# Attention feeding a SiLU feed-forward layer: the keys loaded a second time as plain rows, their root moved into exp's scale, the queries' root and row scaling moved from VectorE to GpSimd

## The chip, the cores and the metric

The kernel runs on one core of a Trainium2 chip. A core has a matrix engine (TensorE, PE in the profile, with its weight loads as PEld), three engines for elementwise work (VectorE = DVE, ScalarE = ACT, GpSimd = POOL) and queues that start DMA transfers (SyncE = SP issues nearly all of them here). Each engine works through its own instruction list strictly in order; engines wait for each other through semaphores. The metric is the device time of one execution in microseconds (us). Three runs of the kernel before gave 1366.65 to 1367.55 us, with a median of 1367.14 us.

## The reference

Inputs are `q`, `k`, `v` of 8 batches x 12 heads x 448 positions x 64, two gain vectors of 64, and two weight matrices of 768 x 2048 and 2048 x 768, all float32.

```
q_n = q / sqrt(mean(q*q, -1) + 1e-6) * g_q        # likewise k_n with g_k
scores = q_n @ k_n.T / sqrt(64)                   # per batch and head
attn = softmax(scores)                            # over the keys
x = (attn @ v), heads side by side                # 3584 x 768
h = x @ w_in ;  g = h * sigmoid(h) ;  out = g @ w_out
```

A query row's root is a factor common to a row of the scores; a key row's root is a factor common to a column. With the keys of one block lying on the 128 partitions, as the scores are computed here (transposed, keys on partitions, queries along the free dimension), the root of a key is one number per partition.

## The kernel before, in words

**Groups.** Four heads (two pairs) of one batch make a group `c`; there are 24 (`NC`), and six of them (`GROUP = 6`) cover two batches. The main loop in `bounded` alternates `visit(c)`, the attention matmuls of a group, and `between(c)`, the preparation of the next group together with two "fills". A fill (`fill`, line 1302) issues matmuls of the first feed-forward product for two batches already finished, done as seven products instead of eight (`Seven`, lines 856 to 893: sums of the inputs, sums of the results), and deals other work (`others`, `prompt`) out between these matmuls at even distances. After the last group a long tail does the rest of the feed-forward products; attention and fills take the first 770 us or so.

**Order.** Everything is under a manual schedule: the instruction order on each engine is the order of the Python calls. PSUM tiles of `scores` and of `scale` come from one pool `sc` with two buffers, each used by the next that asks; those of the products from a pool `mm` with two.

**Early groups (c < 6).** Keys are loaded as plain rows (`load_k`). `normalise` squares them on ACT, sums on DVE (`Norm.squares`, lines 449 and 450), and `Norm.root` makes `1/sqrt` with one DVE instruction (line 474) and a power by POOL (line 478, exponent -0.5). The keys' root is not multiplied into the rows: line 712 gives it to ACT's exp as its scale, one number per partition. The transposes run on PE.

**Late groups (c >= 6), on which the change bears.** q and k are loaded as 32-wide "quarters" (`load_quarters`, line 245, eight DMAs each), so that DVE can transpose them by 32 x 32 blocks (`flip`, lines 636 and 639). For a group c+1 this happens before:

- `sum_squares` (lines 654, 655): ACT squares 128 x 896, DVE sums 28 columns, once for q, once for k; the sums hold half a head each.
- `scale(c + 1)` (lines 660 to 686), called in the middle of `visit(c)`: a small PE matmul adds the two halves (line 664; `ident` was altered by `pair_up` for that), DVE adds epsilon (line 665), then a Newton iteration for the reciprocal root on DVE, ten instructions on 128 x 56 (lines 669 to 678), then two DVE multiplications of 128 x 896 (line 686), which scale the rows of q and of k in place.
- in `between(c)`: `flip(c + 1, "q")` first, then during the second fill `flip(c + 1, "k")` and `gain`, which multiplies by the gains on ACT (line 645).

Exp's scale is then the constant 1.0. Per late group DVE also adds the weights of the softmax (`add`, line 758), inverts the sums (line 787) and combines products (line 828); during groups 5 to 10 it converts and sums pieces of `w_in` too (lines 124 to 131 and 825/828), with POOL's addition on line 135.

The line that the change alters in the exp, and the place where `scale` stood:

```
scale=norm.column(c, i, h, j) if c < GROUP else 1.0,     # line 714, in scores
if GROUP - 1 <= c < NC - 1 and c != GROUP:               # line 1404, in visit
    scale(c + 1)
```

Of the kernel before, what the change touches and what calls it, by code (L numbers as in the profile page):

```python
# [23 lines left out]


SCORE_MAX = 60.0

RSQRT_START = float(0x5F375A86)

BANK = 512  # L30

# [160 lines left out]
def kernel(  # L192
# [60 lines left out]
    def load_q(c, t, steps=1):  # L253
# [7 lines left out]
        for i in range(steps):  # L261
            n = 4 // steps
            dst = t[0:R, ts(i, nq // steps)].rearrange("p (n j d) -> p n (j d)", n=n, j=J)
            nc.sync.dma_start(dst, rows[ts(i, n)].rearrange("n (p j) d -> p n (j d)", j=J))

    def load_k(c):
        t = place[f"k{c % 2}"]
        if c >= z.NPAIR:
            b, cp = divmod(c, z.NPAIR // 2)
            load_quarters(k[b, ts(cp, 4)], t)  # L270
            return
        main, left = keys_of(k, c)
        for i, start in enumerate((z.KA, z.KB)):
            dst = t[:, ds(start, z.KL)].rearrange("p (j h d) -> p j h d", j=z.KEYS, h=2)
            nc.sync.dma_start(dst, main[:, ts(i, 2)].rearrange("p h j d -> p j h d"))
            if i == 0:
                for m in range(2):
                    dst = t[ds(m * z.LEFT, z.LEFT), ds(z.KL, 2 * D)]
                    nc.sync.dma_start(dst.rearrange("p (h d) -> p h d", h=2), left[m])

    def plain_v(c, i):

        b, cp = divmod(c, z.NPAIR // 2)
        rows = v[b, ds(4 * cp + 2 * i, 2)]
        start = i * z.LEFT
        main = rows[:, ds(start, z.KEYS * P)].rearrange("h (j p) d -> p h j d", p=P)
        return main, rows[:, ds((1 - i) * z.KEYS * P, z.LEFT)].rearrange("h p d -> p h d")

    def load_v(c):
        if c >= z.NPAIR:  # L290
            dst = place["v"].rearrange("p (i h j d) -> p i h j d", i=2, h=2, d=D)
            for i in range(2):
                for h in range(2):
                    source = plain_v(c, i)[0][:, h, 0 : z.KEYS - 1]
                    nc.sync.dma_start(dst[:, i, h], source)
            return
        main, _ = keys_of(v, c)
        dst = place["v"].rearrange("p (n j d) -> p n j d", n=4, j=z.KEYS - 1)
        nc.sync.dma_start(dst, main[:, :, 0 : z.KEYS - 1])

    def load_v_rest(c):
        if c >= z.NPAIR:
            for i in range(2):
                main, left = plain_v(c, i)
# [12 lines left out]
    loads = {"q": load_q, "k": load_k, "v": load_v, "vrest": load_v_rest}  # L317

    pairs = [(b, hp) for b in range(z.B) for hp in range(z.NPAIR)]

# [9 lines left out]


    room = Room(nc, const, w_in, z)
    rms = [const.tile([P, 56], F32, name=f"rms{i}") for i in range(2)]
# [97 lines left out]
class Norm:  # L431
# [3 lines left out]
    def __init__(self, nc, z, rms, minus_half):  # L435
        self.nc, self.z, self.rms, self.minus_half = nc, z, rms, minus_half
        self.nq = 2 * z.J

        self.at = [(2 * self.nq, 2 * z.KEYS + 2), (2 * self.nq + 2 * z.KEYS + 2, 2 * z.KEYS)]

    def column(self, c, i, h, j):

# [75 lines left out]
def bounded(  # L518
# [100 lines left out]
    def transpose_k(c):  # L619


        assert z.KB == BANK
        t = ps.tile([P, 2, BANK], F32, name="sc", bufs=2)
        rows = place[f"k{c % 2}"]
        for i in range(2):
            for j in range(z.KEYS + 1 - i):
                nc.tensor.transpose(t[:, i, ts(j, P)], rows[:, ds((z.KA, z.KB)[i] + j * P, P)], ident)
        columns = t.rearrange("p i s -> p (i s)")[:, 0 : z.NK]
        nc.scalar.activation(kT, columns, AF.Copy, scale=gains)
        if c + 2 < NC:  # L630
            loads["k"](c + 2)

    def flip(c, name):

        if name == "q":
            nc.vector.transpose(qT.rearrange("p i s -> p (i s)"), q_of(c)[:, 0 : z.NK])
            load_q(c + 1)
            return
        nc.vector.transpose(kT, place[f"k{c % 2}"])
        if c + 2 < NC:  # L640
            loads["k"](c + 2)

    def gain():

# [1 line left out]

    n = z.NK // z.Q

    def sum_squares(c, name):

        if c >= NC:
            return
        rows = q_of(c)[:, 0 : z.NK] if name == "q" else place[f"k{c % 2}"]
        nc.scalar.activation(squares, rows, AF.Square)  # L654
        nc.vector.tensor_reduce(  # L655
            out=norm.rms[c % 2][:, ts("qk".index(name), n)],
            in_=squares.rearrange("p (n e) -> p n e", e=z.Q), axis=AX.X, op=ALU.add,
        )

    def scale(c):  # L660

        f = norm.rms[c % 2][:, 0 : 2 * n]
        t = ps.tile([P, 2, BANK], F32, name="sc", bufs=2)[:, 0, 0 : 2 * n]
        nc.tensor.matmul(t, ident, f, start=True, stop=True)
        nc.vector.tensor_scalar(
            out=f, in0=t, scalar1=1.0 / D, scalar2=1e-6, op0=ALU.mult, op1=ALU.add
        )
        y, a = (squares[:, ts(i, 2 * n)] for i in range(2))
        nc.vector.tensor_scalar(
            out=y.bitcast(I32), in0=f.bitcast(I32), scalar1=-0.5, scalar2=RSQRT_START,  # L670
            op0=ALU.mult, op1=ALU.add,
        )
        for i in range(3):
            nc.vector.tensor_tensor(out=a, in0=f, in1=y, op=ALU.mult)
            nc.vector.scalar_tensor_tensor(
                out=a, in0=a, scalar=-0.5, in1=y, op0=ALU.mult, op1=ALU.mult
            )
            nc.vector.scalar_tensor_tensor(
                out=f if i == 2 else y, in0=a, scalar=1.5, in1=y, op0=ALU.add, op1=ALU.mult
            )  # L680
        for i, name in enumerate("qk"):
            rows = q_of(c)[:, 0 : z.NK] if name == "q" else place[f"k{c % 2}"]
            rows = rows.rearrange("p (n e) -> p n e", e=z.Q)
            factor = f[:, ts(i, n)]
            factor = factor.rearrange("p (n one) -> p n one", one=1).to_broadcast([P, n, z.Q])
            nc.vector.tensor_tensor(out=rows, in0=rows, in1=factor, op=ALU.mult)

    def pair_up():

# [8 lines left out]
    def scores(c, j, i=None):  # L698
# [12 lines left out]
        for h in range(2):  # L711
            nc.scalar.activation(  # L712
                eleft[:, h] if j == LEFT else weights(c, j)[:, i, h], two[:, h, 0:S], AF.Exp,
                scale=norm.column(c, i, h, j) if c < GROUP else 1.0,
            )

    def turn(step, copy):
# [88 lines left out]
    def normalise(c):  # L806


        def piece(name, i):
            if name == "q":  # L810
                norm.squares_q(c, raw_of(c), scratch[i], i)
                norm.root(c, name, i)
                norm.scale(c, raw_of(c), q_of(c), i, nc.gpsimd)
                if i == 1 and c + 2 < GROUP:
                    load_q(c + 2)
            else:
                norm.squares_k(c, place[f"k{c % 2}"], scratch[i], i)
                if i == 1:
                    norm.root(c, name)

        return [lambda a=a: piece(*a) for a in (("q", 0), ("q", 1), ("k", 0), ("k", 1))]


# [539 lines left out]
    def visit(c):  # L1363

        if c < GROUP - 1:
            beside = normalise(c + 1)
        elif c <= GROUP:
            beside = [lambda: sum_squares(c + 1, "q")]
        else:
            beside = []  # L1370
        if c < NC:
# [29 lines left out]
                loads["vrest"](c + 1)  # L1401
        if c == NC:
            return
        if GROUP - 1 <= c < NC - 1 and c != GROUP:
            scale(c + 1)
        scores(c, 1, 0)
        scores(c, 1, 1)
        if c < GROUP:
# [2 lines left out]
        scores(c, 2, 0)  # L1411
        weigh(c, 1, 1)
        turn(0, nc.scalar.copy)
        if c == GROUP:
            scale(c + 1)
        if c < GROUP:
            run_all(beside[3:4])
        scores(c, 2, 1)
# [11 lines left out]
    def between(c):  # L1430
# [38 lines left out]
        if c % GROUP == GROUP - 1:  # L1469
# [247 lines left out]
```

## Time and profile before

| what | value |
|---|---|
| median of three runs | 1367.14 us |
| the profiled execution's own time | 1367.57 us |
| its span, first to last instruction | 1365.7 us |
| mean granted TensorE clock | 0.991 of full speed |
| PE busy | 1308.2 us, 96% |
| DVE busy | 1017.1 us, 74% |
| ACT busy | 476.5 us, 35% |
| POOL busy | 202.3 us, 15% |
| bytes moved by DMA | 139.42 MB |

"Busy" is the union of an engine's instructions. A group of instructions is given by line, engine and operation, with the tile written, the tiles read, their shapes, the count, then the busy time and the mean duration; after a second bar stands the idle time of the engine just before these instructions, and what ended it. The matrix engine's matmuls are pipelined and overlap in the records, so four matmuls of 64 x 64 on different parts of the array count once; an idle PE is a real loss, while a busy one isn't a proof of full speed.

### The profile page before, as it was taken

How to read it: one execution, taken by the hardware profiler on the slowest of the kernel's cores; microseconds unless marked ns; L12 is line 12 of the kernel's file. 1: busy time of each engine (PE TensorE's matmuls, PEld its weight loads, DVE VectorE, ACT ScalarE, POOL GpSimd, SP SyncE). 2: the span in 40 equal slices, each digit the busy share in tenths (PEclk: the TensorE clock that was granted, in tenths of full speed). 3: DMA queues.
4: the chain of work that ended last, by engine and by line, in shares of the span. 5: the costliest groups of instructions: out<-in, count | busy, mean ns of one | idle time of the engine just before them, and what ended most of it. 6: DMA issues, size and time to landing. Idle time of an engine off the chain costs nothing.

```text
span 1365.7 us, 19617 instructions
## 1 busy us (share of the span) xinstructions
PE 1308.2 (96%) x7111; PEld 811.8 (59%) x7111; DVE 1017.1 (74%) x1810; ACT 476.5 (35%) x859; POOL 202.3 (15%) x169
## 2 busy tenths in 40 slices
PE   8988898899999999999999999999999999999998
PEld 4333333334344444344444455556999999999998
DVE  5787987787766666776665667679887787878785
ACT  7864445454444444444444234420000000000000
POOL 6751111121001000100100134430000000000000
PEclk9998999999999999999999999999999999999999
DMA  9564355433333333333331247531413232323311
GB/s 243 146 149 111 75 134 141 100 77 79 97 85 76 78 100 77 97 78 79 78 91 46 99 130 236 185 123 43 128 45 126 73 97 74 102 76 101 112 59 38
DMA packets 252558, 139.42 MB, mean 102 GB/s; under 512 B 190436, under 2 KB 236388, under 8 KB 252452
## 3 DMA queue, kind: packets, MB, share of 16 engines
q1 hardware_dynamic: 251888, 137.09, 36.0%
q8 instruction: 58, 0.95, 0.3%
q0 software_dynamic: 256, 0.79, 0.2%
q14 instruction: 48, 0.39, 0.1%
q10 hardware_dynamic: 308, 0.20, 0.1%
HBM read 88.47 MB, written 41.29 MB: 95 GB/s over the span
## 4 chain that ended last, share of the span: by engine, by line
PE 50%; DVE 1%; issue 0%; ACT 0%; ACTq 0%; DVEq 0%
PE alone L1177 22%; PE mm L870 8%; PE mm L1177 7%; PE alone L870 7%; PE alone L1214 2%; PE av L744 1%; PE sc L707 1%; PE mm L1214 1%; DVE work L828 0%; PE sc L778 0%; DVE x L828 0%; DVE x L802 0%; DVE rows L825 0%; DVE sums_x L825 0%; DVE work L787 0%
## 5 line engine op out<-in xcount | busy, mean ns | idle before, releaser
L870 PE MATMUL mm<-x,W 128*128 128x448 f32 x636 | 260.9, 552 | 17.3 <-DVE parts L828 8.1
L870 PEld LDWEIGHTS mm<-x,W 128*128 128x128 f32 x636 | 118.1, 192 | 152.2 <-issue 116.7
L870 PE MATMUL mm<-sums_x,W 128*128 128x448 f32 x456 | 185.9, 547 | 5.1 <-DVE stage L828 3.8
L707 PE MATMUL sc<-work 64*64 64x448 f32 x1344 | 163.6, 555 | 14.4 <-ACT work L712 10.1
L712 ACT ACTIVATE work<-sc 128x448 f32<-128x448 f32 x252 | 122.4, 540 | 113.5 <-PE sc L707 90.2
L744 PE MATMUL av<-work,rows 64*64 64x448 f32 x1296 | 147.1, 543 | 7.3 <-DVE av L720 4.3
L870 PEld LDWEIGHTS mm<-sums_x,W 128*128 128x128 f32 x456 | 85.6, 191 | 97.6 <-issue 84.7
L758 DVE TENSOR_TENSOR work<-work 128x896 f32<-128x896 f32 (+1 forms) x114 | 124.0, 1111 | 8.3 <-PE av L744 7.7
L890 POOL TENSOR_TENSOR parts<-parts,stage 128x448 f32<-128x448 f32 x31 | 41.5, 1340 | 489.6 <-DVE parts L828 489.6
L1177 PE MATMUL alone<-W,rows 128*128 128x192 f32 x608 | 113.0, 326 | 0.0
L707 PEld LDWEIGHTS sc<-work 64*64 64x64 f32 x1344 | 46.8, 134 | 97.5 <-issue 31.4
L1177 PEld LDWEIGHTS alone<-W,rows 128*128 128x128 f32 x608 | 101.2, 190 | 0.0
L744 PEld LDWEIGHTS av<-work,rows 64*64 64x64 f32 x1296 | 51.5, 134 | 83.5 <-issue 45.1
L1177 PE MATMUL alone<-W,work 128*128 128x192 f32 x382 | 72.2, 326 | 0.0
L787 DVE RECIPROCAL work<-sc 128x224 f32<-128x224 f32 x36 | 55.7, 1549 | 18.9 <-PE sc L778 18.9
L1008 ACT ACTIVATE stage<-stage 128x896 f32<-128x896 f32 x63 | 57.3, 945 | 34.3 <-DVE stage L828 33.6
L505 POOL DMA_DIRECT2D out_dram<-x x2 | 1.3, 652 | 443.2 <-DVE x L828 443.2
L1177 PEld LDWEIGHTS alone<-W,work 128*128 128x128 f32 x382 | 63.8, 190 | 0.0
L655 DVE TENSOR_REDUCE rms<-rows 128x28 f32<-128x896 f32 x36 | 39.0, 1082 | 31.7 <-ACT rows L654 31.7
L1187 ACT COPY rows<-alone 128x192 f32<-128x192 f32 x34 | 10.8, 318 | 137.5 <-PE alone L1177 79.0
L870 PE MATMUL alone<-x,W 128*128 128x448 f32 x132 | 53.7, 551 | 1.4 <-DVE x L802 1.4
L1191 ACT COPY rows<-alone 128x192 f32<-128x192 f32 x34 | 10.8, 319 | 123.1 <-PE alone L1177 119.6
(248 smaller groups left out, 2144.1 us busy)
## 6 DMA issues: line engine op xcount, KB each, us to landing
hidden<-stage SPq DMA_DIRECT2D x63, 448.0 KB, 2.8
work<-hidden SPq DMA_DIRECT2D x21, 1024.0 KB, 5.1
rows<-in_moe_w_out_dram SPq DMA_DIRECT2D x32, 384.0 KB, 3.4
W<-in_moe_w_in_dram SPq DMA_DIRECT2D x22, 512.0 KB, 4.6
work<-work SPq DMA_DIRECT2D x144, 56.0 KB, 1.9
rows<-in_q_dram SPq DMA_DIRECT2D x144, 56.0 KB, 2.2
rows<-in_k_dram SPq DMA_DIRECT2D x144, 56.0 KB, 2.3
x<-hidden SPq DMA_DIRECT2D x7, 1024.0 KB, 5.5
```

The costliest lines, as they stand in the source:

```text
L655: nc.vector.tensor_reduce(out=norm.rms[c % 2][:, ts("qk".index(name), n)], in_=squares.rearrange("p (n e) -> p n e", e=z.Q), axis=AX.X, op ...
L707: nc.tensor.matmul(two[ds(half * D, D), h, 0:S], keys[rows, ts(half, D)], qT[rows, pair, :], start=True, stop=True,)
L712: nc.scalar.activation(eleft[:, h] if j == LEFT else weights(c, j)[:, i, h], two[:, h, 0:S], AF.Exp, scale=norm.column(c, i, h, j) if c < ...
L744: nc.tensor.matmul(sums[i][ds(h * D, D), :], v, w, start=(j == 0 and step == 1), stop=(j == LEFT - 1 and step == 1),)
L758: nc.vector.tensor_tensor(out=total, in0=total, in1=more, op=ALU.add)
L787: nc.vector.reciprocal(out=r[0][:, rows], in_=t[:, rows])
L870: nc.tensor.matmul(t, self.left(name, s), self.right(name, s), start=s == ends[0], stop=s == ends[1])
L890: nc.gpsimd.tensor_tensor(out=u2, in0=u2, in1=p5, op=ALU.add)
L1008: nc.scalar.activation(t, t, AF.Silu)
L1177: nc.tensor.matmul(t, x[:, i], y, start=i == ORDER[0], stop=i == ORDER[-1])
L1187: nc.scalar.copy(p1, product(1))
L1214: nc.tensor.matmul(o, a[:, 2 * i + m, t], right_one(name, i)[:, m], start=n == 0, stop=n == len(steps) - 1,)
```

## The change

For late groups the keys are now kept twice. The raw quarters go to the buffer `k1` (`load_k_quarters`) and are transposed unscaled; the plain rows go to `k0` (`load_k`, new branch), where only their squares are taken, with the early groups' functions, and their root becomes exp's scale. `scale` now does q alone: matmul and epsilon as before, then POOL's power and POOL's multiplication of the rows; the Newton chain is gone. `scale(c + 2)` is called at the end of `between(c)` instead of `scale(c + 1)` within `visit(c)`. The key's squares for c + 2 stand last in the first fill, behind all softmax additions, where the sum of the k quarters stood between them before.

```
-            load_quarters(k[b, ts(cp, 4)], t)
+            t = place["k0"]
+            for i, start in enumerate((z.KA, z.KB)):
+                main, left = plain(k, c, i)
+                dst = t[:, ds(start, z.KL)].rearrange("p (j h d) -> p h j d", j=z.KEYS, h=2)
+                for h in range(2):
+                    nc.sync.dma_start(dst[:, h], main[:, h])
+                dst = t[ds(i * z.LEFT, z.LEFT), ds(z.KL, 2 * D)]
+                nc.sync.dma_start(dst.rearrange("p (h d) -> p h d", h=2), left)
...
+    def load_k_quarters(c):
+        b, cp = divmod(c, z.NPAIR // 2)
+        load_quarters(k[b, ts(cp, 4)], place["k1"])
...
-        nc.vector.transpose(kT, place[f"k{c % 2}"])
-        if c + 2 < NC:
-            loads["k"](c + 2)
+        nc.vector.transpose(kT, place["k1"])
+        if c + 1 < NC:
+            loads["quarters"](c + 1)
...
     def scale(c):
-        f = norm.rms[c % 2][:, 0 : 2 * n]
+        f = norm.rms[c % 2][:, 0:n]
...
-        for i in range(3):
-            nc.vector.tensor_tensor(out=a, in0=f, in1=y, op=ALU.mult)
...
-        for i, name in enumerate("qk"):
...
-            nc.vector.tensor_tensor(out=rows, in0=rows, in1=factor, op=ALU.mult)
+        nc.gpsimd.tensor_tensor(out=f, in0=f, in1=minus_half.to_broadcast([P, n]), op=ALU.pow)
+        rows = q_of(c)[:, 0 : z.NK].rearrange("p (n e) -> p n e", e=z.Q)
+        factor = f.rearrange("p (n one) -> p n one", one=1).to_broadcast([P, n, z.Q])
+        nc.gpsimd.tensor_tensor(out=rows, in0=rows, in1=factor, op=ALU.mult)
...
-                scale=norm.column(c, i, h, j) if c < GROUP else 1.0,
+                scale=norm.column(c, i, h, j),
...
-                norm.squares_k(c, place[f"k{c % 2}"], scratch[i], i)
+                late = c >= GROUP
+                rows = place["k0" if late else f"k{c % 2}"]
+                norm.squares_k(c, rows, scratch[0 if late else i], i)
                 if i == 1:
                     norm.root(c, name)
+                    if late and c + 1 < NC:
+                        loads["k"](c + 1)
...
-        elif c <= GROUP:
-            beside = [lambda: sum_squares(c + 1, "q")]
+        elif c == GROUP - 1:
+            beside = [lambda: sum_squares(c + 1), lambda: scale(c + 1)] + normalise(c + 1)[2:]
...
-        if GROUP - 1 <= c < NC - 1 and c != GROUP:
-            scale(c + 1)
...
-        keys = [lambda: sum_squares(c + 2, "k")] if c >= GROUP - 2 else []
-        queries = [lambda: sum_squares(c + 2, "q")] if c >= GROUP else []
-        fill(late[:2] + keys + late[2:] + weights_in(c, 0) + [lambda: None])
+        further = normalise(c + 2)[2:] if c >= GROUP - 1 else []
+        queries = [lambda: sum_squares(c + 2)] if c >= GROUP - 1 else []
+        fill(late + weights_in(c, 0) + further)
...
+        if c >= GROUP - 1:
+            scale(c + 2)
```

More of the change, by code (lines that the diff above doesn't have):

```diff
@@ L26 @@
 SCORE_MAX = 60.0
-RSQRT_START = float(0x5F375A86)
 BANK = 512
@@ L268, in load_k @@
         if c >= z.NPAIR:
-            b, cp = divmod(c, z.NPAIR // 2)
-            load_quarters(k[b, ts(cp, 4)], t)
+            t = place["k0"]
[6 more added lines that the diff above has]
+                nc.sync.dma_start(dst.rearrange("p (h d) -> p h d", h=2), left)
             return
@@ L279, in load_k, with plain @@
                     nc.sync.dma_start(dst.rearrange("p (h d) -> p h d", h=2), left[m])
-    def plain_v(c, i):
+    def plain(source, c, i):
         b, cp = divmod(c, z.NPAIR // 2)
-        rows = v[b, ds(4 * cp + 2 * i, 2)]
+        rows = source[b, ds(4 * cp + 2 * i, 2)]
         start = i * z.LEFT
@@ L293, in load_v @@
                 for h in range(2):
-                    source = plain_v(c, i)[0][:, h, 0 : z.KEYS - 1]
+                    source = plain(v, c, i)[0][:, h, 0 : z.KEYS - 1]
                     nc.sync.dma_start(dst[:, i, h], source)
@@ L303, in load_v_rest @@
             for i in range(2):
-                main, left = plain_v(c, i)
+                main, left = plain(v, c, i)
                 dst = place[f"vlast{c % 2}"][:, ts(i, 2 * D)]
@@ L315, in load_v_rest @@
             nc.sync.dma_start(dst.rearrange("p (h d) -> p h d", h=2), left[m])
-    loads = {"q": load_q, "k": load_k, "v": load_v, "vrest": load_v_rest}
+    loads = {"q": load_q, "k": load_k, "quarters": load_k_quarters, "v": load_v, "vrest": load_v_rest}
     pairs = [(b, hp) for b in range(z.B) for hp in range(z.NPAIR)]
@@ L332 @@
     room = Room(nc, const, w_in, z)
-    rms = [const.tile([P, 56], F32, name=f"rms{i}") for i in range(2)]
+    rms = [const.tile([P, 42], F32, name=f"rms{i}") for i in range(2)]
     spare = rows[:, ds(at, 3 * J * D)]
@@ L437, in __init__ @@
         self.nq = 2 * z.J
-        self.at = [(2 * self.nq, 2 * z.KEYS + 2), (2 * self.nq + 2 * z.KEYS + 2, 2 * z.KEYS)]
+        n = z.NK // z.Q
+        self.at = [(n, 2 * z.KEYS + 2), (n + 2 * z.KEYS + 2, 2 * z.KEYS)]
     def column(self, c, i, h, j):
@@ L629, in transpose_k @@
         nc.scalar.activation(kT, columns, AF.Copy, scale=gains)
-        if c + 2 < NC:
-            loads["k"](c + 2)
+        loads["k" if c < GROUP - 1 else "quarters"](min(c + 2, GROUP))
     def flip(c, name):
@@ L638, in flip @@
             return
-        nc.vector.transpose(kT, place[f"k{c % 2}"])
-        if c + 2 < NC:
-            loads["k"](c + 2)
+        nc.vector.transpose(kT, place["k1"])
+        if c + 1 < NC:
+            loads["quarters"](c + 1)
     def gain():
@@ L647, in bounded, with sum_squares @@
     n = z.NK // z.Q
-    def sum_squares(c, name):
+    def sum_squares(c):
         if c >= NC:
             return
-        rows = q_of(c)[:, 0 : z.NK] if name == "q" else place[f"k{c % 2}"]
-        nc.scalar.activation(squares, rows, AF.Square)
+        nc.scalar.activation(squares, q_of(c)[:, 0 : z.NK], AF.Square)
         nc.vector.tensor_reduce(
-            out=norm.rms[c % 2][:, ts("qk".index(name), n)],
-            in_=squares.rearrange("p (n e) -> p n e", e=z.Q), axis=AX.X, op=ALU.add,
+            out=norm.rms[c % 2][:, 0:n], in_=squares.rearrange("p (n e) -> p n e", e=z.Q),
+            axis=AX.X, op=ALU.add,
         )
     def scale(c):
-        f = norm.rms[c % 2][:, 0 : 2 * n]
-        t = ps.tile([P, 2, BANK], F32, name="sc", bufs=2)[:, 0, 0 : 2 * n]
+        if c >= NC:
+            return
+        f = norm.rms[c % 2][:, 0:n]
+        t = ps.tile([P, 2, BANK], F32, name="sc", bufs=2)[:, 0, 0:n]
         nc.tensor.matmul(t, ident, f, start=True, stop=True)
@@ L667, in scale @@
         )
[L668 to L672, printed above, removed]
-        for i in range(3):
-            nc.vector.tensor_tensor(out=a, in0=f, in1=y, op=ALU.mult)
[L675 to L680, printed above, removed]
-        for i, name in enumerate("qk"):
[L682 to L686, printed above, removed]
+        nc.gpsimd.tensor_tensor(out=f, in0=f, in1=minus_half.to_broadcast([P, n]), op=ALU.pow)
+        rows = q_of(c)[:, 0 : z.NK].rearrange("p (n e) -> p n e", e=z.Q)
+        factor = f.rearrange("p (n one) -> p n one", one=1).to_broadcast([P, n, z.Q])
+        nc.gpsimd.tensor_tensor(out=rows, in0=rows, in1=factor, op=ALU.mult)
     def pair_up():
@@ L816, in piece @@
             else:
-                norm.squares_k(c, place[f"k{c % 2}"], scratch[i], i)
+                late = c >= GROUP
+                rows = place["k0" if late else f"k{c % 2}"]
+                norm.squares_k(c, rows, scratch[0 if late else i], i)
                 if i == 1:
                     norm.root(c, name)
+                    if late and c + 1 < NC:
+                        loads["k"](c + 1)
+        if c >= NC:
+            return []
         return [lambda a=a: piece(*a) for a in (("q", 0), ("q", 1), ("k", 0), ("k", 1))]
@@ L1413, in visit @@
         turn(0, nc.scalar.copy)
-        if c == GROUP:
-            scale(c + 1)
         if c < GROUP:
```

## The prediction

> **What bounds the kernel now.** First the page's busy times: PE is the bound and almost full, so only its idle time can be won.
>
> ```profile
> PE 1308.2 (96%) x7111; PEld 811.8 (59%) x7111; DVE 1017.1 (74%) x1810; ACT 476.5 (35%) x859; POOL 202.3 (15%) x169
> ```
>
> Then busy time by stretches, cut where each visit begins (columns: stretch, length, busy PE, PEld, DVE, ACT, POOL, PE clock, DMA share, GB/s). These are groups 6 to 11, then 12 and 13. Groups 6 to 11 have the same PE work (175 or 176 instructions):
>
> ```profile
> 129.00:171.86 42.86, 35.31 (x175) 14.35 (x174) 38.77 (x61) 19.06 (x32) 8.04 (x7) 0.96 0.36 87
> 171.86:207.83 35.97, 33.37 (x176) 13.74 (x175) 29.04 (x45) 17.95 (x32) 6.61 (x6) 1.00 0.51 134
> 207.83:248.83 41.00, 34.57 (x175) 14.52 (x174) 29.76 (x45) 19.11 (x32) 6.41 (x6) 0.96 0.49 131
> 248.83:284.54 35.71, 32.82 (x175) 13.97 (x175) 29.42 (x44) 17.86 (x32) 6.07 (x5) 1.00 0.33 82
> 284.54:323.18 38.64, 34.64 (x176) 14.46 (x175) 32.84 (x46) 18.75 (x32) 6.41 (x4) 0.96 0.37 95
> 323.18:355.59 32.41, 32.32 (x175) 14.26 (x174) 22.46 (x34) 14.72 (x24) 4.45 (x4) 1.00 0.35 81
> 355.59:391.88 36.29, 34.31 (x179) 14.68 (x178) 29.48 (x47) 15.68 (x27) 2.22 (x2) 1.00 0.34 77
> 391.88:426.90 35.02, 34.72 (x180) 14.95 (x179) 22.80 (x35) 15.99 (x27) 2.93 (x2) 1.00 0.36 95
> ```
>
> Group 11, where DVE has 22.5 us of work, runs in 32.4 us; groups 6 to 10, with 29 to 39 us of DVE work (weights), lose 10.5 + 3.6 + 8.6 + 3.3 + 6.2 = 32.1 us. From group 12 on the floor is 34.4 us (the shortest such stretch) and a group loses 0 to 1.9 us, 8.5 us over eleven groups. So the prize is some 40 us, mostly between 129 and 324 us. Who is waited for there (view of waits, that window, PE):
>
> ```profile
> PE mm L870 <- DVE parts L828: 5.8, 3, 3.4
> PE mm L870 <- DVE stage L828: 5.6, 5, 2.9
> PE sc L707 <- ACT work L712: 4.9, 5, 1.1
> PE sc L707 <- DVE rms L665: 3.5, 4, 1.2
> PE av L744 <- DVE av L720: 2.7, 1, 2.7
> ```
>
> The timeline of visit 8 shows the mechanism:
>
> ```profile
> 214.27 0.98 PE L707 MATMUL sc<-work 64*64 64x448 f32 x8 [1.10 <-ACT work L712]
> 216.97 0.21 DVE L665 TENSOR_SCALAR rms<-sc 128x56 f32<-128x56 f32 x1
> 217.24 0.98 PE L707 MATMUL sc<-work 64*64 64x448 f32 x8 [1.23 <-DVE rms L665]
> 220.82 2.09 DVE L686 TENSOR_TENSOR rows<-rows,rms 128x896 f32<-128x896 f32 x2
> 222.83 2.09 DVE L758 TENSOR_TENSOR work<-work 128x896 f32<-128x896 f32 x2
> 231.06 4.01 PE L870 MATMUL mm<-sums_x,W 128*128 128x448 f32 x6 [2.87 <-DVE stage L828]
> ```
>
> Line 664's result holds one of two `sc` buffers until busy DVE reads it; meanwhile scores share the other and wait for exp, too. Then the chain and two row multiplications push the softmax additions back, and the fill starves.
>
> **What the Trainium skill says.** "SBUF — State Buffer", Who interferes with whom: GpSimd shares a port pair with VectorE, exclusively and for a whole instruction, when VectorE has two SBUF inputs or a two-port mode. The trace agrees: line 669 took 1.31 us beside POOL's line 135 against 0.19 alone. But beside POOL's power (54.99 to 58.34) lines 758, 124 and 127 kept their usual times, so I let only the row multiplication lock. "ScalarE: Activation LUTs", What ACT_TABLE_LOAD costs, says that a [128,1] pointer operand adds about 93 ns to an ACTIVATE; here it is 640 against 540 ns. "TensorE: Matmul & The Clock Gate", HAM oscillation, says that PE pauses bring its slow clock back; here matmul issue falls from 0.37 to 0.75 us after the pause at 231.06.
>
> **The change part by part.** Durations, by shape:
>
> ```profile
> L712 ACT ACTIVATE work<-sc 128x448 f32<-128x448 f32 x252 | 122.4, 540 | 113.5 <-PE sc L707 90.2 <-DVE work L758 19.5 <-PE mm L870 2.9
> L712 ACT ACTIVATE work<-sc,rms 128x448 f32<-128x448 f32 x72 | 41.2, 640 | 17.6 <-PE sc L707 13.0 <-DVE work L758 2.8 <-DVE x L758 1.9
> L478 POOL TENSOR_TENSOR rms<-rms,minus_half 128x14 f32<-128x14 f32 x5 | 16.8, 3352 | 3.8 <-DVE rms L474 3.6
> L493 POOL TENSOR_TENSOR rows<-x,rms x4: 1042/1042/1043, 33.1 to 69.6; 112x512 f32<-112x512 f32 x4
> ```
>
> *DVE.* Removed per group: line 669, nine instructions of 0.22 us and two of 1.09, in the timeline 502.35 to 506.92, 4.6 us. The sum over k (1.08) becomes two (0.62 + 0.53 in the early groups) and an epsilon of 0.17, +0.2 us. In groups 11 to 22 the chain costs PE little: DVE would wait anyway, as the additions at 507.31 wait 0.38 us for PE. In groups 6 to 10 it stands on the path.
>
> *POOL, not shown at this width.* The power on 128x28: by the mean cost per column of 128x14, 6.7 us; by the slope from 112x8 (1.63) to 128x14, 7.4; by the same power law, 8.1. I take 6.8 and keep 6.5 to 8.1. Multiplication of 896 at 1.04/512: 1.8 us. With PE's matmul (0.43), line 665's twin (0.2) and handovers, q's rows are ready some 10 us after the fill's end; `flip` needs them 12.3 us after the visit's start in groups 13 and later, 15 to 17 in groups 6 to 9. Hidden by the visit, 2 us to spare. k's root adds a power of 3.35 us, needed a visit later, and delays line 890 by 1 us at most.
>
> *Group 5 to 6 is exposed.* There `scale(6)` stays in the visit: its epsilon at 112.4, then power and multiplication to 121.7, while `flip` stood at 119.73. The inversions move 2 us, and with them PE's wait at 124.9 (2.4 us). Then PE meets `scale(7)` before visit 6; q's sum for it ends near 135 (134.84 before), whereas the old visit had done 3.1 us of work before standing at 134.97. Together 3.6 us late. Visit 6 then gets back line 665's wait (0.7) and the fill's wait at 154.07 (3.45). Net -0.6.
>
> *sc buffers.* In the new place line 665's twin has the 2.2 us of scores and weighted sums before the buffer is needed. Groups 7 to 10 win the visit waits 1.12+0.79, 1.10+1.23, 1.10+0.83, 0.24+0.44+1.10; fill waits 0.66, 2.87, half of 0.96, half of 1.16+1.06; slow clock after two pauses (ten issues or fewer at 0.37 extra), 1.6 and 1.5. Group 10 pays 0.8: q's sum ended 0.6 us after its visit began, and PE now waits for it. Sums: 2.6, 6.8, 2.4, and 4.4 - 0.8 = 3.6. Groups 12 and 18: waits 0.44+1.15+0.35, half of it won (`sum_x` stands ahead of the epsilon): 2.0. Line 665's 0.23 in nine groups: 2.1.
>
> *Exp.* +0.1 us on 14 exps a group. A pair takes 1.16 instead of 0.98 us. A visit with the pointer and no `scale` ran 11.6 us less 0.36 for another wait (42.58 to 54.18); one without pointer 11.56 less 0.66 for `scale` (496.98 to 508.54). So 0.34 us on PE per visit, times 18 groups = 6.1 us lost; bounds 0 and 0.17 x 7 = 1.2 per visit (21 us).
>
> *SP and DMA.* Six more issues per group (v's like ones: 1.92 for four, 0.65 each for two), 3.2 us on SP, behind the squares of k and ahead of the spreading of the inverses, where SP was idle from 514.4 to 524.4. If that cover were gone, line 802 would wait up to 3 us. 459 KB a group, 8 MB in 139, for a DMA share of 0.3: nothing. k's quarters lose their second buffer; loaded after one flip and read at the next, 35 us later. ACT squares k in two parts sharing one scratch, so DVE stands about 1 us between its sums; it idled 1.06 us before line 787 at 520.73. Nothing.
>
> Sum: 0.6 + 2.6 + 6.8 + 2.4 + 3.6 + 2.0 + 2.1 - 6.1 = 14.0 us. From 1367.6 of the profiled execution that gives 1353.6; the median lies 0.4 lower: 1353 us.
>
> **Rivals.**
> - *Eaten by exp* (0.20): each visit loses nearer 0.8 us: 14.4 instead of 6.1, so 1361. For it: ACT exps are among PE's waits already. Against: visits with pointers ran well.
> - *Deeper win* (0.16): half waits and groups 12 to 22 go too, since the additions no longer stand behind k's sum and its wait for ACT (10.0 us of DVE idle on line 655 in 129 to 324): 14 more, 1339.
> - *Slower: POOL's multiplication meets the additions* (0.14). If the power takes 9.3 us or more (above my bound), the multiplication begins beside line 758, the lock lets both additions first, `flip` comes 2 us late in 17 groups and PE loses 1 to 2 of that: 17 to 34 us against 14 won, 1370 to 1388. For it: the estimate is an extrapolation. Against: even 8.1 is met.
> - *Nothing changes* (0.05): heavy groups bound by the weights' DVE work alone, 1367.
>
> The likeliest, 0.45: its own range 1346 to 1358.
>
> **How the numbers follow.** Predicted 1353. The range 1338 to 1369 holds likeliest, eaten, nothing and most of deeper; it leaves out 0.14 slower and some 0.05. Within 0.2% (2.7 us, about what a measurement of this kernel can tell) 0.05; slower 0.15; faster 0.80.
>
> **What would show it.** Right: stretches of groups 7 to 10 near 33 to 36 us, waits for the old line 665 gone; stretches from 13 on unchanged within 0.5 us; exp 640 ns throughout; POOL's power near 6.8 us, ending before the additions. Wrong: the transpose of q waiting for POOL after group 6; PE waiting on the small matmul in every group; exp ending more PE waits than before; DVE idle in fills behind the sums of k.

## The result and the profile after

The changed kernel takes 1345.07 us (median of four runs, 1343.86 to 1346.0); the kernel before, run beside it, 1366.89 us. The ratio is 0.984, with a 95% interval of 0.9823 to 0.9857: 21.8 us faster, where 14 were forecast. The profiled execution took 1346.0 us, its span is 1344.1 us. The page's busy times show what left VectorE (DVE, 65 us less) and what came to GpSimd (POOL, 167 us more); PE has the same 7111 matmuls and is 97% full:

```profile
PE 1300.4 (97%) x7111; PEld 828.3 (62%) x7111; DVE 951.8 (71%) x1630; ACT 502.3 (37%) x877; POOL 369.5 (27%) x223
```

Busy time by stretches, cut again where each visit's first scores begin, groups 6 to 12 (columns: stretch, length, busy PE, PEld, DVE, ACT, POOL, PE clock, DMA share, GB/s):

```profile
131.36:168.85 37.49, 35.03 (x175) 15.59 (x174) 30.05 (x45) 17.86 (x29) 15.32 (x9) 0.93 0.49 118
168.85:203.38 34.53, 32.93 (x175) 14.92 (x174) 26.76 (x36) 20.12 (x33) 16.60 (x9) 1.00 0.60 152
203.38:243.42 40.04, 34.44 (x175) 15.65 (x174) 27.17 (x35) 20.57 (x34) 16.73 (x9) 0.96 0.55 144
243.42:276.84 33.42, 32.61 (x175) 15.02 (x175) 28.00 (x35) 20.23 (x33) 15.18 (x8) 1.00 0.44 106
276.84:313.09 36.25, 32.74 (x175) 15.09 (x174) 29.30 (x35) 18.91 (x31) 16.43 (x8) 1.00 0.44 111
313.09:345.73 32.64, 32.41 (x176) 15.07 (x175) 18.41 (x24) 16.11 (x25) 13.48 (x7) 1.00 0.42 96
345.73:380.03 34.30, 33.73 (x179) 15.91 (x179) 27.10 (x37) 17.30 (x28) 11.50 (x5) 1.00 0.43 96
```

Group 6 is 5.4 us shorter, but group 5 ahead of it is 5.3 us longer (the second small matmul now stands before visit 6's first scores, so it counts to group 5): nothing. Groups 7 to 10 are 1.4, 1.0, 2.3 and 2.4 us shorter, 7.1 together, half of what was forecast; group 8 still takes 40.04 us. Where the rest is, the visits' starts tell: visit 5 begins at 103.36 instead of 106.28 (2.9 us, from group 4's fills, which the prediction left out: the sum of group 6's keys has moved from there to visit 5), and groups 12 to 22 take 374.15 instead of 386.50 us (12.3 us, where the prediction's terms come to a gain of 0.4: 2.0 and 2.1 less eleven times 0.34). So the total was near while its places were not.

The view of waits for 131 to 345 us, PE, has two new entries: the small matmul waiting for q's sum, and products waiting for a copy into `stage` on ScalarE (line 888):

```profile
PE mm L870 <- DVE parts L828: 7.0, 6, 2.0
PE sc L673 <- DVE rms L662: 4.5, 2, 3.9
PE mm L870 <- DVE stage L828: 3.5, 5, 1.0
PE mm L870 <- ACT stage L888: 3.2, 2, 2.5
```

In this stretch the waits of scores for the old line 665 and for exp are gone. One ordinary visit, first in the kernel before, then after, shows what that is worth (timeline, columns: start, length, engine, line, operation, wait):

```profile
465.19 0.43 PE L664 MATMUL sc<-rms,ident 128*128 128x56 f32 x2
465.60 2.04 PE L707 MATMUL sc<-work 64*64 64x448 f32 x16
471.57 2.09 DVE L758 TENSOR_TENSOR work<-work 128x896 f32<-128x896 f32 x2 [0.36 <-PE av L744]
```

```profile
452.08 1.72 PE L701 MATMUL sc<-work 64*64 64x448 f32 x16
457.92 2.09 DVE L752 TENSOR_TENSOR work<-work 128x896 f32<-128x896 f32 x2 [4.44 <-PE av L738]
```

In the kernel before, the small matmul and the 16 matmuls of scores after it take 2.27 us, from 465.19 to the next weighted sums at 467.46; after, the 16 alone take 1.54, from 452.08 to 453.62. Besides its own time the small matmul holds one of the two `sc` buffers until VectorE has read it (line 665, at 466.39). No single gap there is above 0.25 us, so the list of waits hardly has it. The last lines of the two views are the softmax additions: before, they followed a chain of 4.6 us and waited 0.36 us for PE; now VectorE is idle for 4.44 us ahead of them.

Group 8's remaining loss (timeline of the changed kernel) is a queue of work:

```profile
226.22 0.90 SPq L903 DMA_DIRECT2D hidden<-stage  x2
229.50 0.53 ACT L888 COPY stage<-mm 128x448 f32<-128x448 f32 x1 [8.56 <-DMA hidden<-stage]
230.08 2.52 PE L870 MATMUL mm<-x,W 128*128 128x448 f32 x6 [2.55 <-ACT stage L888]
231.31 0.52 ACT L458 ACTIVATE rows<-rows 128x384 f32<-128x384 f32 x1 [0.75 <-DVE rms L459]
232.54 1.55 DVE L781 RECIPROCAL work<-sc 128x224 f32<-128x224 f32 x1
234.62 4.22 PE L870 MATMUL mm<-sums_x,W 128*128 128x448 f32 x6 [2.02 <-DVE parts L828]
```

The save is issued late, behind q's eight loads on SP; ScalarE's copy waits 8.56 us for it, and PE 2.55 us for the copy; k's squares stand behind the copy; the second square waits 0.75 us for VectorE's first sum, since both squares use one scratch; the inversions follow the sums, and PE waits 2.02 us for VectorE. The six new loads of plain key rows are not ahead of the save in this queue: they are issued behind it, from 230.59 to 233.96.

The rows of the new work by shape (columns: busy us, mean ns, idle before it and for whom):

```profile
L706 ACT ACTIVATE work<-sc,rms 128x448 f32<-128x448 f32 x324 | 185.5, 635 | 86.2 <-PE sc L701 62.8 <-DVE work L752 17.7 <-DVE x L752 2.1
L677 POOL TENSOR_TENSOR rms<-rms,minus_half 128x28 f32<-128x28 f32 x18 | 86.2, 4791 | 74.7 <-DVE rms L674 63.3 <-DVE av L714 9.3 <-DMA rows<-in_k_dram 2.2
L458 ACT ACTIVATE rows<-rows 128x384 f32<-128x384 f32 x18 | 9.5, 527 | 43.0 <-DVE rms L459 43.0
```

GpSimd's power takes 4.79 us, not 6.8. And ScalarE's second square stands 43.0 us in all for VectorE's first sum.

### The profile page after: what moved, and what is told of

The parts are those of the page before. It is cut to its first block, busy times and chain, and to the rows that moved or that the text cites. A ratio compares the mean times of both kernels' runs of the same rounds, so it can differ in the third digit from the quotient of the medians.

```text
span 1344.1 us, 19812 instructions
## 1 busy us (share of the span) xinstructions
PE 1300.4 (97%) x7111; PEld 828.3 (62%) x7111; DVE 951.8 (71%) x1630; ACT 502.3 (37%) x877; POOL 369.5 (27%) x223
## 4 chain that ended last, share of the span: by engine, by line
PE 81%; DVE 7%; ACT 4%; DMA 3%; issue 2%; SPq 2%; POOL 0%; ACTq 0%; DVEq 0%
PE mm L870 24%; PE alone L1177 22%; PE av L738 8%; PE sc L701 8%; PE mm L1177 7%; PE alone L870 7%; PE alone L1214 2%; DVE work L781 1%; DVE work L752 1%; DMA rows<-in_k_dram 1%; PE sc L772 1%; SPq L249 1%; DVE sums_x L825 1%; PE mm L1214 1%; ACT L1008 1%
## 5 line engine op out<-in xcount | busy, mean ns | idle before, releaser
L706 ACT ACTIVATE work<-sc,rms 128x448 f32<-128x448 f32 x324 | 185.5, 635 | 86.2 <-PE sc L701 62.8
L701 PE MATMUL sc<-work 64*64 64x448 f32 x1344 | 167.3, 550 | 1.7 <-DVE rms L674 1.1
L738 PE MATMUL av<-work,rows 64*64 64x448 f32 x1296 | 156.0, 546 | 4.7 <-ACT av L714 1.8
L487 POOL TENSOR_TENSOR rms<-rms,minus_half 128x14 f32<-128x14 f32 (+3 forms) x37 | 88.3, 2389 | 134.6 <-DVE rms L483 133.9
L738 PEld LDWEIGHTS av<-work,rows 64*64 64x64 f32 x1296 | 60.7, 133 | 76.0 <-issue 35.4
L677 POOL TENSOR_TENSOR rms<-rms,minus_half 128x28 f32<-128x28 f32 x18 | 86.2, 4791 | 74.7 <-DVE rms L674 63.3
L701 PEld LDWEIGHTS sc<-work 64*64 64x64 f32 x1344 | 55.5, 134 | 69.1 <-ACT work L706 26.9
L1187 ACT COPY rows<-alone 128x192 f32<-128x192 f32 x34 | 10.9, 320 | 137.4 <-PE alone L1177 78.9
L459 DVE TENSOR_REDUCE rms<-rows 128x8 f32<-128x512 f32 (+2 forms) x48 | 30.2, 629 | 40.3 <-ACT rows L458 37.5
```

The lines of the kernel that those rows point to most:

```text
L487: nc.gpsimd.tensor_tensor(out=t, in0=t, in1=half, op=ALU.pow)
L677: nc.gpsimd.tensor_tensor(out=f, in0=f, in1=minus_half.to_broadcast([P, n]), op=ALU.pow)
L701: nc.tensor.matmul(two[ds(half * D, D), h, 0:S], keys[rows, ts(half, D)], qT[rows, pair, :], start=True, stop=True,)
L706: nc.scalar.activation(eleft[:, h] if j == LEFT else weights(c, j)[:, i, h], two[:, h, 0:S], AF.Exp, scale=norm.column(c, i, h, j),)
L738: nc.tensor.matmul(sums[i][ds(h * D, D), :], v, w, start=(j == 0 and step == 1), stop=(j == LEFT - 1 and step == 1),)
```

## The experiments

In each run the stretches between the visits' starts were taken from its profile (us; the last column is the span from visit 23's start, which no edit aims at, and which varies by 5 us all the same, so small differences of medians are read with the stretches; visit 5, too, begins anywhere from 101.6 to 103.6 in the changed kernel and the eight runs made from it, all alike up to there):

| run | median | visit 5 begins | groups 5 to 11 | groups 12 to 22 | rest |
|---|---|---|---|---|---|
| kernel before | 1367.9 | 106.3 | 249.3 | 386.5 | 623.6 |
| changed kernel | 1345.1 | 103.4 | 242.4 | 374.2 | 624.2 |
| two scratches | 1340.7 | 103.6 | 237.9 | 373.6 | 623.8 |
| pointer alone | 1372.3 | 106.3 | 249.7 | 390.9 | 622.7 |
| constant again | 1339.7 | 102.1 | 241.5 | 371.0 | 623.5 |
| order alone | 1359.3 | 102.7 | 245.4 | 388.0 | 621.7 |
| q on VectorE | 1363.0 | 101.6 | 246.3 | 386.3 | 627.0 |
| q on VectorE, early | 1366.6 | 101.9 | 247.2 | 389.4 | 625.6 |
| one power more | 1363.8 | 102.4 | 254.6 | 381.2 | 623.6 |
| two powers more | 1466.3 | 101.6 | 290.6 | 447.7 | 624.1 |
| two scratches, seven later | 1340.7 | 102.5 | 238.5 | 373.6 | 625.4 |
| the same, one square | 1342.2 | 102.1 | 240.0 | 373.2 | 625.7 |

My theory after reading the traces: the removal of the small matmul and its chain from the visit holds the late groups' gain, the later sum of k the early ones', and the shared scratch took part of it back. The rivals are in each expectation.

**The shared scratch, undone.**

```diff
-                norm.squares_k(c, rows, scratch[0 if late else i], i)
+                norm.squares_k(c, rows, squares[:, ds(512 * i, 512 - 128 * i)] if late else scratch[i], i)
```

> The changed kernel, with one edit: the two square pieces of k in the late groups write two separate scratch stretches instead of the same one. Theory A (the shared scratch makes ScalarE's second square wait for VectorE's first sum, and this lateness is what took 7 us of the 15 us hoped for in groups 7 to 10): the 43 us of idle time in front of the 128x384 square fall to nearly nothing and the time falls by 3 to 7 us, to 1338 to 1342 us. Rival B (the alternation lies off the path; groups 7 to 10 lose to a late save and a late copy behind weight loads): the idle time goes and the time stays within 0.2%, 1343 to 1347 us.

1340.67 us, ratio to the kernel before 0.9797 (0.978 to 0.9813): 4.4 us below the changed kernel. The same row as above lost its idle time:

```profile
L458 ACT ACTIVATE rows<-rows 128x384 f32<-128x384 f32 x18 | 9.3, 519 | 0.0
```

Groups 7, 8 and 10 give 0.7, 2.6 and 0.5 us, so 3.8 of the 4.4. Theory A holds, though not for all of the 7 us that were missing: of 43 us of idle time, some 4 lay on the path, where VectorE was late already. In group 8 PE's waits become only about 1.1 us shorter; the larger part is a slow clock (0.60 for 4.3 us) that followed the wait of 2.02 us, and does not follow the 1.33 us left of it. Group 8 keeps its wait for the late save.

**The pointer, in both directions.** The kernel before with a pointer, then the changed kernel without:

```diff
-                scale=norm.column(c, i, h, j) if c < GROUP else 1.0,
+                scale=norm.column(c, i, h, j) if c < GROUP else ones[:, 0, 0:1],
```

> The kernel before, with one edit: the late groups' exps take their scale from a column (of ones) instead of the constant 1.0. The prediction's step (6.1 us lost, 0.34 us in each of 18 visits): about 1373 us, with exps of about 635 ns. Rival (the exps' extra time is hidden beside the matmuls and VectorE's additions): 1366 to 1368 us.

1372.26 us, ratio 1.0038 (1.0023 to 1.0053): 4.4 us lost, all of it in groups 12 to 22, but not 0.34 us a visit: ordinary visits there are about 0.2 us longer, and visits 12 and 18 alone take 2.6 us more (15.79 and 14.71 instead of 13.96 and 13.90).

```diff
-                scale=norm.column(c, i, h, j),
+                scale=norm.column(c, i, h, j) if c < GROUP else 1.0,
```

> The changed kernel, with one edit: the late groups' exps take the constant 1.0 as scale again, so k's root is left out of their scores and the output is not the reference's. If the pointer costs 0.34 us in each of 18 visits as predicted: about 1339 us. If the exps are hidden: 1344 to 1346 us.

1339.68 us, ratio 0.979 (0.9773 to 0.9806): 5.4 us less than the changed kernel. An ordinary visit takes 10.68 us from its first scores to the first product, 10.98 with the pointer: 0.30 us each, 5.4 if all 18 paid it. The stretches show 4.1 in groups 5 to 22: groups 6, 9 and 10 get nothing, since what the visit wins is waited for in the fill. (Visit 5 begins 1.2 us earlier, where the two kernels are alike.) So the exps are not hidden; the prediction's 0.34 a visit was near, its 6.1 somewhat high.

**The order of k's sum alone.**

```diff
-        fill(late[:2] + keys + late[2:] + weights_in(c, 0) + [lambda: None])
+        fill(late + weights_in(c, 0) + keys + [lambda: None])
```

> The kernel before, with one edit: k's square and sum stand behind all additions and weight work in the first fill, not between the additions. Theory O (the sum between the additions is what made the first fills' waits, and what made groups 12 to 22 about 1.1 us longer each): 1353 to 1361 us. Rival (only the root chain's removal from VectorE shortened them; the order is worth nothing or is worse, since k's sum now runs into the inversions): 1365 to 1372 us.

1359.26 us, ratio 0.9928 (0.9912 to 0.9945): 8.6 us for one line's order by the medians, 6.0 by the stretches up to visit 23; within what theory O said, but not where it said. (The empty piece that closed the list falls away too.) Visit 5 begins 3.6 us earlier: in group 4's second fill PE's wait for a product's copy, 3.89 us at 103.00 before, is 1.90 us at 100.95, and the four products behind it take 1.77 us instead of 3.35. Group 8 is 4.0 us shorter (37.05), and its clock is back at 1.00. Groups 12 to 22 are 1.5 us longer. So the order explains group 4 and group 8, and nothing of the 12.3 us.

**q's half undone.** The chain of ten steps on VectorE and its row multiplication, inside the visit, with k as changed (the chain's body is that of the kernel before on 28 columns):

```diff
-        nc.gpsimd.tensor_tensor(out=f, in0=f, in1=minus_half.to_broadcast([P, n]), op=ALU.pow)
+        y, a = (squares[:, ts(i, n)] for i in range(2))
...
-        nc.gpsimd.tensor_tensor(out=rows, in0=rows, in1=factor, op=ALU.mult)
+        nc.vector.tensor_tensor(out=rows, in0=rows, in1=factor, op=ALU.mult)
...
-            beside = [lambda: sum_squares(c + 1), lambda: scale(c + 1)] + normalise(c + 1)[2:]
+            beside = [lambda: sum_squares(c + 1), lambda: None] + normalise(c + 1)[2:]
...
+        if GROUP - 1 <= c < NC - 1 and c != GROUP:
+            scale(c + 1)
         scores(c, 1, 0)
...
+        if c == GROUP:
+            scale(c + 1)
         scores(c, 2, 1)
...
-        if c >= GROUP - 1:
-            scale(c + 2)
```

> The changed kernel with q's part undone: q's root is made by the chain of ten small steps on VectorE (28 columns instead of 56), q's rows are multiplied by VectorE, and both are called inside the visit where they stood in the kernel before; k stays changed (loaded twice, roots in the exps' scale, sum behind the additions). Theory Q (q's half of the change holds about half of the gain: a small matmul and its line in the middle of each visit cost 0.6 us in each of 17 visits, about 10 us, and the chain delays the copies and additions on VectorE): 1354 to 1364 us. Rival K (k's half, one row multiplication of 1.09 us less and the later sum, holds nearly all): 1344 to 1350 us. Rival N (without q's part the change is worth nothing, its gain from the order being paid back to the pointer and the shared scratch): 1365 to 1370 us.

1363.0 us (1358.96 to 1363.82), ratio 0.9948 (0.993 to 0.9966). The time lies in theory Q's range, but q's half is worth much more than the half of the gain that Q gave it: 18 us by the medians, 16.1 by groups 5 to 22 (632.6 instead of 616.5). Of k's half, 3.2 us lie in these groups, and 3 to 5 ahead of visit 5. Groups 12 to 22 take 386.3 us, as in the kernel before, but not in the same places: their visits take 136.0 us (132.1 in the kernel before, 122.5 in the changed one), their fills 250.2 (254.4 in the kernel before, 251.7 in the changed one). So k's half wins 4.1 us in these fills and pays 3.9 in the visits, where the pointer is, and the 12.3 us are, in the net, q's half: 13.5 won in the visits. Group 8 takes 36.9 us here, with the shared scratch and the new loads in place; in the changed kernel its visit is 3.1 us shorter, and the fill behind it 6.3 us longer.

**The place alone, without GpSimd.** The same chain on VectorE, called at the fill's end (edit against the run above):

```diff
-            beside = [lambda: sum_squares(c + 1), lambda: None] + normalise(c + 1)[2:]
+            beside = [lambda: sum_squares(c + 1), lambda: scale(c + 1)] + normalise(c + 1)[2:]
...
-        if GROUP - 1 <= c < NC - 1 and c != GROUP:
-            scale(c + 1)
         scores(c, 1, 0)
...
-        if c == GROUP:
-            scale(c + 1)
         scores(c, 2, 1)
...
+        if c >= GROUP - 1:
+            scale(c + 2)
```

> The changed kernel, its q chain on VectorE as in the run above, but called at the end of the second fill, where the changed kernel calls it: the place alone, without GpSimd. Theory Q in the form that the place is what counts (the small matmul leaves the visit's middle): within 3 us of the changed kernel, 1343 to 1348 us. Rival V (about 3.2 us of chain and multiplication now stand on VectorE ahead of the copy that turns the banks and of the divisions, so the second products of each visit wait some 1 to 1.5 us, 17 times): 1362 to 1372 us.

1366.64 us, ratio 0.9991 (0.9984 to 0.9997): 3.6 us more than with the chain in its old place, so the place alone wins nothing. Timeline of one visit:

```profile
460.54 1.09 DVE L692 TENSOR_TENSOR rows<-rows,rms 128x896 f32<-128x896 f32 x1 [0.22 <-DMA rows<-in_k_dram]
461.76 0.98 PE L750 MATMUL av<-work,rows 64*64 64x448 f32 x8 [0.70 <-DVE av L726]
```

The multiplication ends at 461.6; only then comes the copy that turns the banks, and PE has waited 0.70 us for it. A visit takes 11.9 us instead of 10.98 (rival V; its wait is 0.7 us and not 1 to 1.5). So the early place pays only with another engine to do the work there. GpSimd in the old place was not run, nor was the small matmul moved without its chain; what the matmul costs by itself is read from the timelines.

**GpSimd's slack, by one power more and by two.**

```diff
...
+        for _ in range(1):
+            nc.gpsimd.tensor_tensor(
+                out=own["unread"], in0=f, in1=minus_half.to_broadcast([P, n]), op=ALU.pow
+            )
         nc.gpsimd.tensor_tensor(out=f, in0=f, in1=minus_half.to_broadcast([P, n]), op=ALU.pow)
```

> The changed kernel with one more power of 128x28 on GpSimd ahead of q's own in each late group, into a tile that nothing reads. In the trace of the changed kernel q's rows are ready about 4.7 us before the flip takes them, and one power is 4.79 us. If only that slack counts: 1344 to 1348 us. If GpSimd's row multiplication, now beside the visit's additions, slows VectorE (the prediction's slower case): 1352 to 1370 us.

1363.77 us, ratio 0.9971 (0.996 to 0.9982): 18.7 us more than the changed kernel, lost to a power that should just have fitted. GpSimd and VectorE in one visit:

```profile
470.99 2.18 POOL L685 TENSOR_TENSOR rows<-rows,rms 128x896 f32<-128x896 f32 x1
```

```profile
470.52 3.60 DVE L757 TENSOR_TENSOR work<-work 128x896 f32<-128x896 f32 x2 [4.43 <-PE av L743]
474.04 1.10 DVE L645 STREAM_TRANSPOSE work<-rows 128x896 f32<-128x896 f32 x1
475.07 0.58 DVE L833 TENSOR_TENSOR stage<-mm,parts 128x448 f32<-128x448 f32 x1
```

The two additions, 2.09 us in the changed kernel, take 3.60 beside GpSimd's multiplication; transpose and recombination behind them are 1.5 us late, and PE waits 1.33 us for the recombination at 475.70. That is the prediction's slower rival, made real by a chain of 9.6 us; it fits what "SBUF — State Buffer", Who interferes with whom, of the Trainium skill says of the port pair that the two engines share: a VectorE instruction with two inputs in SBUF contends with a GpSimd instruction that reads SBUF. It is so in eleven of the 18 visits, where the second addition takes 2.58 us instead of, mostly, 1.08. In six others (5, 7, 9, 11, 12, 18) the additions are done before the multiplication starts, and the flip waits for GpSimd itself, 14.7 us in all. In an ordinary visit of the changed kernel the multiplication ends at 455.22 and the additions begin at 457.92: the slack there is those 2.7 us, not the 4.7 to the flip. Of the loss, 12.2 us lie in groups 5 to 11.

> The changed kernel with two more powers of 128x28. The flip must then come about 4.9 us late in each of 17 late groups; everything on VectorE behind the flip (additions, recombinations) is as late. If the fill has no cover for it, 40 to 85 us more: 1385 to 1430 us. If the fill's matmuls and its work behind cover half of it or more: 1347 to 1380 us.

(The same loop with range(2).) 1466.31 us, ratio 1.0718 (1.07 to 1.0735): 121 us more than the changed kernel, beyond the 85 expected. The flip waits for GpSimd 106.7 us in all, and where PE then waits it pays once more (timeline, and the windows view of the stretch behind the wait):

```profile
415.54 4.85 PE L875 MATMUL mm<-sums_x,W 128*128 128x448 f32 x6 [4.44 <-DVE stage L833]
425.92 2.42 PE L875 MATMUL mm<-sums_x,W 128*128 128x448 f32 x6
```

```profile
415.54:421.00 5.46, 5.46 (x8) 2.71 (x9) 3.24 (x4) 0.58 (x2) 0.00 (x0) 0.55 0.52 96
```

After a wait of 4.44 us the granted clock is 0.55 for some 5 us, and six matmuls take 4.85 us that take 2.42 ten us later. In the view of waits (105 to 900 us) PE's waits sum to 26.2 us in the changed kernel and to 112.4 here. My expectation counted these 86 us, and left out the clock, to which I put most of the other 35.

**Two attempts at a better version.** Both build on the two scratches.

```diff
-        if c >= GROUP - 1:
+        if c >= GROUP:
             scale(c + 2)
...
+        if c == GROUP:
+            scale(c + 1)
         scores(c, 1, 0)
```

> The changed kernel with two edits: the two scratch stretches of the run with that edit alone (1340.7 us), and q's chain of group 7 called in visit 6 after its first four products, where the matmul need not hold up the visit for q's late sum (4.08 us at 130.80 in the changed kernel). If the wait goes and GpSimd still has q's rows of group 7 ready for the flip: 1336 to 1338 us. If the rows then come too late for the flip and the wait moves into group 6's first fill: 1339 to 1344 us.

1340.74 us, ratio 0.9799 (0.9783 to 0.9816): no difference. Group 5 is 5.5 us shorter and group 6 is 6.2 longer: the wait of 4 to 5 us goes from the small matmul to the bank-turning copy on VectorE at 131.38. So it was not q's sum alone that was late: weights and sums of the fill's end keep VectorE busy, with short waits for ScalarE's squares, until 131 us, and whatever stands first behind them waits. Neither expectation named that.

```diff
-                norm.squares_k(c, rows, squares[:, ds(512 * i, 512 - 128 * i)] if late else scratch[i], i)
+                if not late:
+                    norm.squares_k(c, rows, scratch[i], i)
+                elif i == 1:
+                    norm.squares(rows, squares, norm.rms[c % 2][:, ds(n, n // 2)])
```

> The run above, with k's two square pieces and two sums of each late group made one square of 896 columns and one sum of 28/2 columns (the scratch is then q's own). If only the number of instructions on ScalarE and VectorE counts in the fill: 0.5 to 2 us less than the run above. If one long sum (about 1.08 us) holds VectorE in front of a product's evacuation where two short ones let it in between: 0.5 to 3 us more.

1342.16 us, ratio 0.9808 (0.9792 to 0.9824): 1.4 us more than the run above, with overlapping intervals; fewer instructions are at any rate no gain. The run with two scratches alone is as good as any of the complete kernels here, 1340.67 us.

## Why the prediction was right, and where its steps were not

The time lay inside the range, 8 us below the likeliest value and 1 us below the likeliest case's own range. The range was wide, and held no change at all as well. That the total came near is in part luck: half of what groups 7 to 10 were to give did not come, and groups 4 and 12 to 22 gave 15 us that the sum did not have. Of its own signs, line 665's waits did go; but the stretches from 13 on, which were to stay within 0.5 us, fell by 0.2 to 2.2, and group 8 stayed at 40.

- *Groups 7 to 10 (15.4 us in the sum).* Measured 7.1; the pointer, which the prediction counts apart, takes 0.6 here. The step that failed is the sentence on the two squares sharing one scratch, costed at nothing: 4.4 us, 3.8 of them here. Its cover was one group's idle 1.06 us in front of the inversions; in the groups where VectorE was late there was none. With two scratches these groups give 10.8 us, some 11.4 without the pointer (an estimate: the two were not taken out together), so 4 of the 15.4 stay open. Most of that is group 8, the largest term (6.8), which gave 1.0, and 3.6 with two scratches. Its fill's wait of 2.87 us was put down to the chain, but falls to 1.31 by the order of k's sum alone; and in the changed kernel the rest of its waits follow a save queued behind q's loads on SP, which was queued so in the kernel before, too, but held nothing up there.
- *"In groups 11 to 22 the chain costs PE little", with "line 665's 0.23 in nine groups: 2.1" and "groups 12 and 18: 2.0".* This is the mis-sized term. Without the pointer an ordinary visit fell from 11.59 to 10.68 us, 0.91 and not 0.23, so 8.2 in nine; visits 12 and 18 fell from 13.96 and 13.90 to 11.51 and 11.49, 4.9 and not 2.0. I had read the list of waits, which shows what waits visibly, where the timeline of the visit against a visit without the small matmul shows the whole. The small matmul, moved to the fill's end, takes 0.30 us there. The floor of 34.4 us that was taken for these groups was not one: it had the small matmul in it, and in the changed kernel all eleven take 33.5 to 34.3.
- *Exp (−6.1).* Right in kind, somewhat high: 5.4 by the medians and 4.1 by the stretches when taken out; 4.4 when put in alone, there mostly in visits 12 and 18.
- *Group 5 to 6 (net −0.6).* Near (−0.1), with its wait of 3.9 us where forecast; the cause is VectorE's work at the fill's end, not the position of q's sum.
- *POOL (6.8 us for the power, hidden).* Hidden, with 4.79 us; below the lower bound of 6.5, since cost per column was carried over from narrower tiles. The slower rival did not come, but its mechanism is real with twice the power, in eleven visits, and the loss there (18.7 us, of which late rows are a part) lies in the 17 to 34 foreseen.
- *Left out:* k's sum gone from group 4's fill and behind the additions elsewhere: the order alone gave 6.0 to 8.6 us. The diff moves it; I had taken a sum of one engine's work and not the place in the queue. The deeper rival counted it, for the fills of groups 12 to 22, where the order alone gives 0.8 us and their visits lose 2.3. Those groups won 9.6 us in visits and 2.7 in fills.
- *SP and DMA at nothing:* no run tests it; in the trace k's first squares, which read the plain rows, start with 0.0 us of idle time before them.

## What to carry to other kernels

A small instruction in the middle of a dense stretch on the bounding engine can cost more than the waits listed for it: measure the stretch against one without it. Here moving such a chain earlier paid only with another engine to do it, and that engine's slack ended, in most visits, where its two-input instruction met VectorE's, not where its result was read. And scratch shared by two engines' pieces was free only where both had time; it was not where the kernel was latest. What a visit wins is kept only if the fill behind it does not wait for another queue.

## What the hardware did that I had not expected

- A power on GpSimd does not scale with its columns as I had worked out: 128x28 took 4.79 us in all 18 groups, while 128x14 took 3.35 us in the early groups and mostly 2.58 in the late ones, for the same shape. Why is open.
- The slow clock after a long wait (0.55 for about 5 us behind 4.44 us of waiting) adds some 2.4 us to the price of that wait. "TensorE: Matmul & The Clock Gate", HAM oscillation, of the Trainium skill names the effect, a matrix engine that falls back to its slow clock over waits; here is its size. Below that, the length of the wait did not settle it: behind 2.38 us at group 5 the clock was 0.59 in the changed kernel (122.76 to 126.80), and behind the same wait of 2.38 us it was 1.00 in the run with two scratches (122.96 to 125.40).
